# Opening loads of a Mamba-2 and hard-swish kernel: two issuing queues, and the first weight block decoded ahead of C's transpose

## The chip, the cores and the metric

The kernel runs on one core of a Trainium2 chip. The metric is the device time of one execution in microseconds; the figure given for a kernel is the median of its runs. The profile is one execution, recorded on the same core. Its span runs from the first to the last instruction.

## The reference: what is computed

Two blocks follow each other. The first is a chunked state-space recurrence over 4 batches, 8 heads and 768 tokens, with 32 values and 16 states per head:

```python
log_a = np.log(np.clip(a, 1e-06, 1.0))
for c in range(nc):
    cum = np.cumsum(la, axis=-1)
    L = np.exp(cum[:, :, :, None] - cum[:, :, None, :]) * causal
    CB = np.einsum('bhin,bhjn->bhij', Cc, Bc)
    y_intra = np.einsum('bhij,bhjd->bhid', CB * L, xc)
    y_inter = np.einsum('bhin,bhnd->bhid', Cc, state) * np.exp(cum)[:, :, :, None]
    y[:, :, sl] = y_intra + y_inter
    state = decay_full * state + (sum over j of Bc, xc, decay_from_j)
```

The result, 3072 tokens by 256 features, goes through a feed-forward block with 2048 hidden features:

```python
h = x @ w_in
g = h * np.clip(h + 3.0, 0.0, 6.0) / 6.0
return (g @ w_out).astype(np.float32)
```

The two weight matrices come as 64-bit floats; all other inputs are 32-bit.

## The kernel before, in words

**Tiling.** The sequence is cut into six chunks of 128 tokens; one chunk of all four batches is 512 tokens. For each chunk c the recurrence gives yT (256 features by 512 tokens), and the feed-forward block of group k = c turns it into 512 rows of the output. The recurrence of chunk k + 1 is woven into the feed-forward work of group k. Groups 1 to 5 do both matrix products with seven block products in place of eight, from sums of weights and of activations; group 0 does them plainly (`mlp_in` at L608, `first_out` at L698).

**Order.** Nothing is scheduled automatically: every engine and every DMA queue does its work in the order of the program text. Semaphores between them are put in by the framework. Transfers raise one of eight DMA semaphores in turn, and a transfer whose semaphore is still in use by an earlier one waits for that one to land. In the kernel before, all transfers are issued by SP.

**Weights.** The weights are decoded on the core. Each matrix is loaded in four blocks of 1 MB of raw 64-bit words (`load_w`, L128), into three buffers in turn (`raw`). In the text, w0 to w3 are the blocks of w_in, blocks 4 to 7 those of w_out. `decode(i)` (L188) is a generator of five steps, and `weights(i, n)` takes n of them:

- ScalarE copies the top 16 bits (`ws`, L199); for blocks 0 and 1 VectorE also builds the significand (`wm`, L202 and L206) in this step.
- VectorE cuts exponent and sign (`we`, L216, and `ws`, L218); for later blocks L202 follows.
- ScalarE turns the exponent into a bfloat16 factor (`we`, L222).
- ScalarE does so a second time (L224); for later blocks VectorE does L206; and the load of block i + 3 is issued.
- VectorE adds the sign (L229) and writes the 32-bit weights (`w_in` or `w_out`, L237).

**The opening.** Chunk 0 has a path of its own, since nothing precedes it. SP loads a, w0, C in eight transfers of 32 KB (`pairs_first`, L96), B in one transfer of 4096 pieces of 64 bytes (`tokens_first`, L91), and x in 4096 pieces of 128 bytes. Meanwhile the logarithms of a are taken (L265, L267), added up by a scan (L270) and split into three bfloat16 parts. TensorE forms the decay differences of chunks 0 and 1 in PSUM (`diff`: L349 and L358), and ScalarE takes their exponentials into L (`diff_exp`, L366). C is transposed by VectorE in blocks of 32 (`turn_squares`, L464) and spread over even and odd heads (`part_heads`, L470). B is transposed by TensorE (`turn_b`, L428; ScalarE copies the result to bT, L432) and scaled by GpSimd (`ends`, L392, into `bs`). `scores` (L506) multiplies them into cb, `multiply` (L553) puts cb into L, `mix` (L578) multiplies L with x, and `keep` (L598) copies the result to yT by four copies on ScalarE. `fade` (L477) scales the second half of C by the decay, for the part of `mix` that reads the state in the chunk's middle. `turn_cum` and `by_token` (L315, L319) put the later chunks' decay sums on partitions, through a PSUM bank (`c_ps`, tag f1) that the second half of `mix` writes next.

**Where w1 is asked for.** `load_w(1, behind=...)` at L882 first has GpSimd copy one column of L into the new buffer (L132). So the transfer waits until `multiply` has written that part of L. Blocks 2 and 3 are issued right after.

Of the kernel before, what the change touches and what calls it, by code (L numbers as in the profile page):

```python
# [8 lines left out]
FP32 = mybir.dt.float32  # L9
# [11 lines left out]
def kernel(  # L21
# [63 lines left out]
    def load_bc(c):  # L85

        sl = slice(c * P, (c + 1) * P)

        def tokens_first(src, **where):  # L91
            t = loads.tile([P, NB * NH, N], FP32, **where)
            nc.sync.dma_start(out=t, in_=src[:, :, sl, :].rearrange("b h s n -> s (b h) n"))
            return t

        def pairs_first(src):  # L96
            t = loads.tile([P, 2, NB, 4, N], FP32, name="pairs", tag="bc")
            for b in range(NB):
                for h in range(2):
                    nc.sync.dma_start(  # L100
                        out=t[:, h, b].rearrange("s a n -> s (a n)"),
                        in_=src[b, h:NH:2, sl, :].rearrange("h (s a) n -> h s (a n)", a=4))
            return t

        if c == 0:
            bcs[c] = [pairs_first(C)]
        elif c < TURN:
            bcs[c] = [tokens_first(C, name="C", tag="bc")]
        Bs[c] = tokens_first(B, name="B")
        if c < TURN:  # L110
            bcs[c].append(Bs[c])
        else:
            bcs[c] = [pairs_first(C), pairs_first(B)]

    def load_x(c):
        sl = slice(c * P, (c + 1) * P)
        xts[c] = loads.tile([P, NB * NH, D], FP32, name="xt")
        nc.sync.dma_start(out=xts[c], in_=x[:, :, sl, :].rearrange("b h s d -> s (b h) d"))
# [6 lines left out]
    NRAW = 3  # L125
    raws = {}

    def load_w(i, behind=None):  # L128

        raw = loads.tile([P, NK * FP * 2 * P], U32, name="raw", bufs=NRAW)  # L130
        if behind is not None:
            nc.gpsimd.tensor_copy(raw[:, :1].bitcast(FP32), behind)  # L132
        if i < NP:
            cols = slice(2 * i * FP * P, 2 * (i + 1) * FP * P)
            src = moe_w_in[:, cols].rearrange("(k p) f -> p k f", p=P)
            dst = raw.rearrange("p (k f) -> p k f", k=NK)
        else:
            r0 = (i - NP) * FP * P
            src = moe_w_out[r0:r0 + FP * P, :].rearrange("(k p) m -> p k m", p=P)
            dst = raw.rearrange("p (k m) -> p k m", k=FP)  # L140
        nc.sync.dma_start(out=dst, in_=src)
        raws[i] = raw

    load_w(0)
    load_bc(0)
    load_x(0)
    nc.scalar.preload_act_table_set("natural_log_exp_and_others")


# [38 lines left out]
    def decode(i):  # L188

        n = NK * FP * P
        top = raws[i].bitcast(U16).rearrange("p (n w) -> p n w", w=4)[:, :, 3]
        lo, hi = (raws[i].rearrange("p (n w) -> p n w", w=2)[:, :, w] for w in range(2))
        s = att.tile([P, n], U16, name="ws")
        e = att.tile([P, n], U16, name="we")
        m = att.tile([P, n], U32, name="wm")
        nc.scalar.copy(out=s, in_=top)  # L199

        def significand():
            nc.vector.tensor_scalar(  # L202
                out=m, in0=hi, scalar1=0xFFFFF, scalar2=0x100000,
                op0=ALU.bitwise_and, op1=ALU.bitwise_or)
            yield
            nc.vector.scalar_tensor_tensor(  # L206
                out=m.bitcast(FP32), in0=lo, scalar=2.0 ** -32, in1=m, op0=ALU.mult,
                op1=ALU.add)
            yield

        parts_m = significand()
        if i < 2:
            next(parts_m)
            next(parts_m)
        yield
        nc.vector.tensor_scalar(  # L216
            out=e, in0=s, scalar1=0x7FF0, scalar2=None, op0=ALU.bitwise_and)
        nc.vector.tensor_scalar(  # L218
            out=s, in0=s, scalar1=0x8000, scalar2=None, op0=ALU.bitwise_and)
        next(parts_m, None)  # L220
        yield
        nc.scalar.activation(e.bitcast(BF16), e, AF.Relu, bias=bias_hi, scale=-8.0)  # L222
        yield
        nc.scalar.activation(e, e.bitcast(BF16), AF.Relu, bias=bias_lo, scale=-1.0)  # L224
        next(parts_m, None)
        if i and i + NRAW < 2 * NP:
            load_w(i + NRAW)
        yield
        nc.vector.tensor_tensor(out=e, in0=e, in1=s, op=ALU.bitwise_or)  # L229
        m, e = m.bitcast(FP32), e.bitcast(BF16)  # L230
        if i < NP:
            dst = w_in[:, :, i * FP * P:(i + 1) * FP * P]
            m, e = (t.rearrange("p (k f) -> p k f", k=NK) for t in (m, e))
        else:
            dst = w_out[:, (i - NP) * FP:(i - NP + 1) * FP, :]
            m, e = (t.rearrange("p (k f) -> p k f", k=FP) for t in (m, e))
        nc.vector.scalar_tensor_tensor(  # L237
            out=dst, in0=m, scalar=2.0 ** -20, in1=e, op0=ALU.mult, op1=ALU.mult)
# [30 lines left out]
    def add_up(sl):  # L269
        nc.vector.tensor_tensor_scan(  # L270
            out=cum[:, sl], data0=run.rearrange("g c p -> g (c p)")[:, sl], data1=a_sb[:, sl],
            initial=0.0, op0=ALU.mult, op1=ALU.add)
# [90 lines left out]
    def diff_exp(c, b):  # L363
        if c not in Ls:
            new_decays(c)
        nc.scalar.activation(Ls[c][:, b], ds.pop((c, b)), AF.Exp)  # L366

    def first_eto():

        e_ps = ps.tile([P, NB, HT], FP32, name="e_ps", tag="f0")  # L370
        for b in range(NB):
            nc.tensor.matmul(
                out=e_ps[:, b],
                lhsT=picks[:, b * P:(b + 1) * P],
                rhs=split[:, 0, HALF[1]], start=(b == 0), stop=True, skip_group_check=True)
        etos[0] = att.tile([P, NB, P], FP32, name="eto")
        nc.scalar.activation(etos[0][:, :, HALF[1]], e_ps, AF.Exp)
# [14 lines left out]
    def ends(c, b):  # L392

        if b == 0:
            bss[c] = att.tile([P, G, N], FP32, name="bs")
        hs = slice(b * NH, b * NH + NH)
        nc.gpsimd.tensor_tensor(  # L397
            out=bss[c][:, hs], in0=Bs[c][:, hs],
            in1=Ls[c][:, b, :, HT - 1:HT].to_broadcast([P, NH, N]), op=ALU.mult)
# [8 lines left out]
    def turned(c):  # L408
        if c not in bTs:
            bTs[c] = [att.tile([P, NB, P], FP32, name="bT", bufs=1),  # L410
                      att.tile([P, NB, 2, P], FP32, name="cT", bufs=1),
                      att.tile([P, NB, P], FP32, name="csT", bufs=1)]
        return bTs[c]
# [14 lines left out]
    def turn_b(c):  # L428

        t_ps = turn_ps(c, 1)  # L430
        transposes(c, 1, t_ps)
        nc.scalar.copy(out=turned(c)[0], in_=t_ps)  # L432
# [31 lines left out]
    def turn_squares(t, out):  # L464

        nc.vector.transpose(
            out=out.rearrange("r b (s a) -> r b a s", a=4),
            in_=t.rearrange("s t b a n -> s (b a) t n"))

    def part_heads(c):  # L470
        _, cT, csT = turned(c)
        for t in range(2):
            nc.vector.tensor_scalar(
                out=cT[:, :, t], in0=csT, scalar1=parity[:, t:t + 1], scalar2=None,
                op0=ALU.mult)

    def fade(c, sl=slice(0, P)):  # L477
        csT = turned(c)[2][:, :, sl]
        nc.vector.tensor_tensor(out=csT, in0=csT, in1=etos[c][:, :, sl], op=ALU.mult)

    def turn_all(c):
        bT, _, csT = turned(c)
# [358 lines left out]
    def weights(i, n):  # L841
        for _ in range(n):
            next(parts[i], None)


    def diff(c, *bs):
        for part in (diff_less, diff_pick):
            for b in bs:
                part(c, b)
# [10 lines left out]
        mask_again(0, b)  # L860
    diff(0, 0, 1)
    diff(0, 2, 3)
    turn_squares(bcs[0][0], turned(0)[2])
    part_heads(0)
    for b in range(NB):
        diff_exp(0, b)
    first_eto()
    weights(0, 1)
    add_up(ends_at[1])
    store_rows()  # L870
    diff(1, 2, 3)
    turn_b(0)
    for b in range(NB):
        ends(0, b)
    weights(0, 1)
    diff(1, 0, 1)
    diff_exp(1, 2)
    diff_exp(1, 3)
    weights(0, 2)
    scores(0)  # L880
    multiply(0)
    load_w(1, behind=Ls[0][:, 0, 2, :1])  # L882
    load_w(2)
    load_w(3)
    c_ps = ps.tile([P, NC, G], FP32, name="c_ps", tag="f1")
    turn_cum(c_ps)
    by_token(c_ps)
    busy(1, ps.tile([P, NB * P], FP32, name="d", tag="f0"))
    fade(0, HALF[1])
    weights(0, 1)  # L890
    mix(0)
    keep(0)
    weights(1, 2)
    renew(0)
    weights(1, 3)
    load_eto(1)
    load(1)

# [136 lines left out]
```

## Time and profile before

| what | us |
|---|---|
| median of 3 runs | 363.7 (362.79 to 363.85) |
| profiled execution, its span | 361.1 |
| TensorE matmul busy | 349.9 |
| VectorE busy | 223.3 |
| ScalarE busy | 177.2 |
| GpSimd busy | 139.5 |
| first matmul of the up projection (h, L611) starts | 23.46 |
| first matmul of the down projection (o, L708) starts | 53.77 |

The runs' times are taken without the profiler and include what lies around the span, here 2.6 us between the span and the median. PE is TensorE's matmuls, PEld its weight loads, DVE is VectorE, ACT ScalarE, POOL GpSimd; SPq is SP's queue of transfers. A line of a timeline has the start, the length and the engine, then the line of the code, the operation, output<-inputs and a count, and in brackets how long the engine had been idle before it and what ended that wait. In the chain of waits each piece is released by the one above it.

### The profile page before, as it was taken

The page shows a single profiled execution, that of the slowest core. Times are in us where ns is not written, and L with a number is a line of the kernel's source. Part 1 is how long each engine was busy: PE and PEld are TensorE (multiplying, and loading weights), DVE is VectorE, ACT ScalarE, POOL GpSimd, SP SyncE. Part 2 cuts the span into 40 slices and gives each one's busy share as a digit, 9 for nine tenths or more (in the row PEclk, how much of TensorE's full clock was granted, in tenths as well). Part 3 has the DMA queues.
Part 4 walks back from the last instruction along what each step waited for, and adds up shares of the span by engine and source line. Part 5 has one row for each costly group of instructions (what it writes and reads, how often), then busy time and mean ns, then how long its engine had stood idle before and what let it go on. Part 6 is the DMA issues. An engine that isn't in the chain of part 4 may idle for free.

```text
span 361.1 us, 9354 instructions
## 1 busy us (share of the span) xinstructions
PE 349.9 (97%) x3936; PEld 300.4 (83%) x3936; DVE 223.3 (62%) x427; ACT 177.2 (49%) x390; POOL 139.5 (39%) x139
## 2 busy tenths in 40 slices
PE   7698999999999999999999999999999999999996
PEld 3553438888888999888999888999888999888996
DVE  4778999976787634587435587535588421588111
ACT  4548878439656550575460476470476110476100
POOL 3400000182299712079722079720058700058700
PEclk9699999999999999999999999999999999999999
DMA  5979969901935043560034560000000000000000
GB/s 154 109 270 254 145 230 156 172 2 43 181 55 77 4 98 91 72 93 2 2 76 104 79 96 2 4 2 31 29 2 1 4 2 31 30 3 0 2 29 31
DMA packets 75482, 24.97 MB, mean 69 GB/s; under 512 B 66032, under 2 KB 71824, under 8 KB 74928
## 3 DMA queue, kind: packets, MB, share of 16 engines
q1 hardware_dynamic: 75440, 24.37, 34.7%
q8 instruction: 31, 0.51, 0.6%
q14 instruction: 11, 0.09, 0.1%
HBM read 21.07 MB, written 3.29 MB: 67 GB/s over the span
## 4 chain that ended last, share of the span: by engine, by line
PE 76%; DVE 13%; ACT 4%; DMA 3%; SPq 2%; issue 1%; DVEq 0%; POOL 0%; ACTq 0%
PE ob L767 18%; PE even L653 18%; PE oa L767 18%; PE odd L653 13%; DVE gT L694 2%; DVE wm L206 2%; PE o L708 2%; PE y L589 2%; PE cb L523 2%; PE y L501 2%; ACT we L222 2%; SPq L100 2%; DMA raw<-in_moe_w_in_dram 2%; DMA B<-in_B_dram 1%; DVE w_out L237 1%; DVE we L229 1%
## 5 line engine op out<-in xcount | busy, mean ns | idle before, releaser
L753 POOL TENSOR_TENSOR s<-gT 128x512 f32<-128x512 f32 x20 | 26.4, 1321 | 89.5 <-DVE gT L694 89.5
L653 PE MATMUL even<-ts,w_sum 128*128 128x256 f32 x160 | 48.2, 383 | 0.0
L668 ACT COPY even<-odd 128x512 f32<-128x512 f32 x40 | 23.0, 576 | 48.6 <-PE odd L653 46.3
L689 ACT ACTIVATE gT<-odd,half 128x512 f32<-128x512 f32 x40 | 27.5, 687 | 35.0 <-DVE odd L682 35.0
L653 PE MATMUL odd<-yT,w_in 128*128 128x256 f32 x160 | 41.1, 379 | 0.0
L767 PE MATMUL oa<-w_out,gT 128*128 128x128 f32 x320 | 38.9, 277 | 0.0
L767 PEld LDWEIGHTS oa<-w_out,gT 128*128 128x128 f32 x320 | 38.1, 192 | 0.9
L767 PE MATMUL ob<-w_out,s 128*128 128x128 f32 x320 | 37.4, 275 | 0.0
L767 PEld LDWEIGHTS ob<-w_out,s 128*128 128x128 f32 x320 | 36.5, 192 | 0.0
L653 PEld LDWEIGHTS even<-ts,w_sum 128*128 128x128 f32 x160 | 29.9, 190 | 5.3 <-ACT up L675 1.5
L694 DVE SCALAR_TENSOR_TENSOR gT<-gT,odd 128x512 f32<-128x512 f32 x40 | 27.5, 688 | 9.9 <-ACT gT L689 9.9
L653 PEld LDWEIGHTS odd<-yT,w_in 128*128 128x128 f32 x160 | 30.1, 190 | 3.9
L386 ACT ACTIVATE L<-L,cum_n 128x64 f32<-128x64 f32 x128 | 31.1, 339 | 0.0
L767 PE MATMUL ob<-t,gT 128*128 128x128 f32 x240 | 30.3, 279 | 0.0
L611 PE MATMUL h<-yT,w_in 128*128 128x512 f32 x64 | 28.4, 599 | 1.9 <-DVE gT L694 1.6
L689 ACT ACTIVATE gT<-even,half 128x512 f32<-128x512 f32 x40 | 27.7, 694 | 4.4 <-PE even L653 4.4
L694 DVE SCALAR_TENSOR_TENSOR gT<-gT,even 128x512 f32<-128x512 f32 x40 | 27.1, 679 | 4.4 <-ACT gT L689 4.4
L767 PEld LDWEIGHTS ob<-t,gT 128*128 128x128 f32 x240 | 27.9, 192 | 1.2 <-issue 0.5
L708 PE MATMUL o<-w_out,gT 128*128 128x256 f32 x128 | 28.7, 381 | 0.0
L669 DVE COPY up<-odd 128x256 f32<-128x256 f32 x40 | 17.0, 424 | 18.7 <-ACT even L668 17.9
L708 PEld LDWEIGHTS o<-w_out,gT 128*128 128x128 f32 x128 | 24.0, 190 | 4.0 <-ACT gT L689 0.8
L397 POOL TENSOR_TENSOR bs<-B,L 128x128 f32<-128x128 f32 x24 | 14.5, 612 | 31.6 <-ACT L L386 23.5
(130 smaller groups left out, 614.9 us busy)
## 6 DMA issues: line engine op xcount, KB each, us to landing
raw<-in_moe_w_in_dram SPq DMA_DIRECT2D x4, 1024.0 KB
raw<-in_moe_w_out_dram SPq DMA_DIRECT2D x4, 1024.0 KB
L<-cum_d SPq DMA_DIRECT2D x8, 512.0 KB
xt<-in_x_dram SPq DMA_DIRECT2D x6, 512.0 KB
out_dram<-res SPq DMA_DIRECT2D x20, 128.0 KB
B<-in_B_dram SPq DMA_DIRECT2D x6, 256.0 KB
eto<-cum_e SPq DMA_DIRECT2D x20, 64.0 KB
pairs<-in_C_dram SPq DMA_DIRECT2D x32, 32.0 KB
```

What stands on the lines that cost most here:

```text
L100: nc.sync.dma_start(out=t[:, h, b].rearrange("s a n -> s (a n)"), in_=src[b, h:NH:2, sl, :].rearrange("h (s a) n -> h s (a n)", a=4))
L386: nc.scalar.activation(Ls[c][:, b, h], Ls[c][:, b, h], AF.Exp, bias=cum_n[:, c, g:g + 1])
L397: nc.gpsimd.tensor_tensor(out=bss[c][:, hs], in0=Bs[c][:, hs], in1=Ls[c][:, b, :, HT - 1:HT].to_broadcast([P, NH, N]), op=ALU.mult)
L611: nc.tensor.matmul(out=h.rearrange("p r i -> p (r i)"), lhsT=w_in[:, j, f * P:(f + 1) * P], rhs=yTs[k][:, j].rearrange("p b i -> p (b i)") ...
L653: nc.tensor.matmul(out=bank[:, r], lhsT=lhsT, rhs=rhs, start=start, stop=True, skip_group_check=True)
L668: nc.scalar.copy(out=even, in_=odd[:, 1:2].to_broadcast([P, 2, 2 * P]))
L669: nc.vector.tensor_copy(out=up[:, 1], in_=odd[:, 0])
L689: nc.scalar.activation(gTs[k][:, f], h.rearrange("p r i -> p (r i)"), AF.Relu, bias=half, scale=1.0 / 6.0)
L694: nc.vector.scalar_tensor_tensor(out=g, in0=g, scalar=1.0, in1=h.rearrange("p r i -> p (r i)"), op0=ALU.min, op1=ALU.mult)
L708: nc.tensor.matmul(out=o[:, b % 2], lhsT=gTs[0][:, f, b * P:(b + 1) * P], rhs=w_out[:, f], start=(f == 0 and b % 2 == 0), stop=True, skip_ ...
L753: nc.gpsimd.tensor_tensor(out=o, in0=p_, in1=q_, op=op)
L767: nc.tensor.matmul(out=bank[:, slot], lhsT=lhs[:, j], rhs=rhs[:, j], start=(clear and j == 0), stop=True, skip_group_check=True)
```

## The change

The change has five parts.

- **Two queues.** w0 and chunk 0's B are issued by ScalarE, ahead of its activation table load; a, C, x and then w1 by SP. In SP's order the load of w1 now stands behind x, without the copied column, and the loads of blocks 2 and 3 before and after `scores` and `multiply`.
- **First decoding moved.** Block 0's first two steps of `decode` (ScalarE's copy of the top bits; VectorE's significand, exponent and sign) now stand ahead of the exponentials and of C's transpose. Its third step stands ahead of chunk 1's exponentials.
- **Second block's decoding.** Only block 0 builds its significand in the first step; block 1 does so as the later blocks do. Its first step stands ahead of `keep`, so ScalarE does that copy before the four yT copies. Its next three steps stand between `keep` and `renew`, and the last one behind `renew`.
- **`by_token` moved.** It stands behind block 0's last step.
- **`fade` of chunk 0 moved.** It is done by GpSimd, right behind C's `part_heads` in the text and, on GpSimd, behind the four operations of `ends`.

TensorE's order is the same as before.

```diff
-        def tokens_first(src, **where):
+        def tokens_first(src, queue=nc.sync, **where):
             t = loads.tile([P, NB * NH, N], FP32, **where)
-            nc.sync.dma_start(out=t, in_=src[:, :, sl, :].rearrange("b h s n -> s (b h) n"))
+            queue.dma_start(out=t, in_=src[:, :, sl, :].rearrange("b h s n -> s (b h) n"))
...
+        if 0 < c < TURN:
+            bcs[c] = [tokens_first(C, name="C", tag="bc")]
+        Bs[c] = tokens_first(B, nc.scalar if c == 0 else nc.sync, name="B")
         if c == 0:
-            bcs[c] = [pairs_first(C)]
+            bcs[c] = [pairs_first(C), Bs[c]]
         elif c < TURN:
-            bcs[c] = [tokens_first(C, name="C", tag="bc")]
-        Bs[c] = tokens_first(B, name="B")
-        if c < TURN:
             bcs[c].append(Bs[c])
...
-    def load_w(i, behind=None):
+    def load_w(i, queue=nc.sync):
         raw = loads.tile([P, NK * FP * 2 * P], U32, name="raw", bufs=NRAW)
-        if behind is not None:
-            nc.gpsimd.tensor_copy(raw[:, :1].bitcast(FP32), behind)
...
-        nc.sync.dma_start(out=dst, in_=src)
+        queue.dma_start(out=dst, in_=src)
...
-    load_w(0)
+    load_w(0, nc.scalar)
     load_bc(0)
     load_x(0)
+    load_w(1)
     nc.scalar.preload_act_table_set("natural_log_exp_and_others")
...
         parts_m = significand()
-        if i < 2:
+        if i == 0:
...
-    def fade(c, sl=slice(0, P)):
+    def fade(c, sl=slice(0, P), engine=nc.vector):
         csT = turned(c)[2][:, :, sl]
-        nc.vector.tensor_tensor(out=csT, in0=csT, in1=etos[c][:, :, sl], op=ALU.mult)
+        engine.tensor_tensor(out=csT, in0=csT, in1=etos[c][:, :, sl], op=ALU.mult)
...
     diff(0, 2, 3)
-    turn_squares(bcs[0][0], turned(0)[2])
-    part_heads(0)
+    weights(0, 1)
     for b in range(NB):
         diff_exp(0, b)
     first_eto()
+    diff(1, 2, 3)
     weights(0, 1)
+    for b in range(NB):
+        ends(0, b)
+    turn_b(0)
+    diff(1, 0, 1)
+    weights(0, 1)
+    diff_exp(1, 2)
+    diff_exp(1, 3)
+    turn_squares(bcs[0][0], turned(0)[2])
+    part_heads(0)
+    fade(0, HALF[1], nc.gpsimd)
     add_up(ends_at[1])
     store_rows()
-    diff(1, 2, 3)
-    turn_b(0)
-    for b in range(NB):
-        ends(0, b)
+    load_w(2)
     weights(0, 1)
-    diff(1, 0, 1)
-    diff_exp(1, 2)
-    diff_exp(1, 3)
-    weights(0, 2)
     scores(0)
     multiply(0)
-    load_w(1, behind=Ls[0][:, 0, 2, :1])
-    load_w(2)
     load_w(3)
     c_ps = ps.tile([P, NC, G], FP32, name="c_ps", tag="f1")
     turn_cum(c_ps)
+    busy(1, ps.tile([P, NB * P], FP32, name="d", tag="f0"))
+    weights(0, 1)
+    weights(1, 1)
     by_token(c_ps)
-    busy(1, ps.tile([P, NB * P], FP32, name="d", tag="f0"))
-    fade(0, HALF[1])
-    weights(0, 1)
     mix(0)
     keep(0)
-    weights(1, 2)
+    weights(1, 3)
     renew(0)
-    weights(1, 3)
+    weights(1, 1)
```

## The prediction, made blind

> **What bounds the kernel now.** I read the page first, then the chain of waits in order of time, then the timelines of single queues and engines in the first 80 us, and last a table of DMA and clock by stretch. The page's chain says where the span lies:
>
> ```profile
> PE 76%; DVE 13%; ACT 4%; DMA 3%; SPq 2%; issue 1%; DVEq 0%; POOL 0%; ACTq 0%
> ```
>
> From 77 us on the chain is TensorE without a gap, work that the change doesn't touch. What is to be had lies before it. There the chain runs (start, length, what):
>
> ```profile
> 7.63 5.02 DMA B<-in_B_dram
> ...
> 12.79 1.09 PE t_ps L423 x4
> ...
> 15.72 2.06 PE cb L523 x64
> ...
> 19.14 0.20 POOL raw L132
> ...
> 19.35 5.43 DMA raw<-in_moe_w_in_dram
> ...
> 24.81 0.70 DVE wm L202
> ```
>
> B's landing at 12.65 releases its transposes and, through them, the scores (cb). The scores' end releases the multiplications into L (17.79). Only then is the second weight block (w1) asked for, and it lands at 24.79. B is late because SP's queue issues one transfer after another:
>
> ```profile
> 0.80 0.40 SPq L80 DMA_DIRECT2D pre<-in_a_dram  x1
> 1.26 0.41 SPq L141 DMA_DIRECT2D raw<-in_moe_w_in_dram  x1
> 1.73 5.86 SPq L100 DMA_DIRECT2D pairs<-in_C_dram  x8
> 7.63 0.47 SPq L93 DMA_DIRECT2D B<-in_B_dram  x1
> 8.15 3.28 SPq L118 DMA_DIRECT2D xt<-in_x_dram  x1
> ```
>
> C is as late as B for its own reader, VectorE, which idles 4.43 us ahead of it, while ScalarE copies w0 only after the decay exponentials:
>
> ```profile
> 10.71 1.08 DVE L466 STREAM_TRANSPOSE csT<-pairs 128x512 f32<-128x512 f32 x1 [4.43 <-DMA pairs<-in_C_dram]
> ```
>
> TensorE idles from 10.0 to 12.79, and its clock is halved from 12.0 to 18.7 (columns: stretch, length, busy of PE, PEld, DVE, ACT, POOL, then clock, DMA share, GB/s):
>
> ```profile
> 8.00:10.00 2.00, 2.00 (x71) 1.40 (x70) 0.00 (x0) 1.92 (x5) 0.00 (x0) 1.00 0.94 115
> 10.00:12.00 2.00, 0.01 (x2) 0.00 (x0) 1.26 (x2) 0.85 (x1) 0.00 (x0) 1.00 0.89 69
> 12.00:14.00 2.00, 1.21 (x5) 1.00 (x6) 1.97 (x4) 0.09 (x1) 1.20 (x2) 0.50 1.17 175
> ```
>
> From 23.46 TensorE does the first group's up projection (h), then its down projection (o), which ends near 75.6:
>
> ```profile
> 23.46 7.13 PE L611 MATMUL h<-yT,w_in 128*128 128x512 f32 x16
> 32.17 14.14 PE L611 MATMUL h<-yT,w_in 128*128 128x512 f32 x32 [1.58 <-DVE gT L694]
> 46.67 7.13 PE L611 MATMUL h<-yT,w_in 128*128 128x512 f32 x16 [0.36 <-DVE w_in L237]
> 53.77 15.78 PE L708 MATMUL o<-w_out,gT 128*128 128x256 f32 x72
> ```
>
> Two gaps stand in it, 1.58 and 0.36, both waits for the decoded weights. VectorE's chain (decoding, gT) and TensorE's arrive together at 75.7, where csT is ready. So the whole must gain on both: TensorE from an earlier start of h and from the gaps, VectorE from an earlier w1.
>
> **What the Trainium skill says.** "DMA: Bandwidth & Descriptors", section "Issuing engines are not separate DMA queues": transfers of all queues run on the same 16 DMA engines, and a second queue saves only issue time. The trace agrees that issue is what costs: the ten transfers from C on take until 11.43 to issue. Section "Queues, rings and completion order" there: the DMA engines take turns between queues by packet; all early loads of this trace are on one queue, so it isn't shown. "TensorE: Matmul & The Clock Gate", section "What's actually happening": the clock halves after an idle window of about 3.4 us. Here 2.0 us of idle were enough (10.0 to 12.0), and the measurement counts. "SBUF — State Buffer", section "SBUF: two separate sides": GpSimd and a VectorE operation with two SBUF inputs exclude each other; bs (L397) took 587 to 1390 ns each beside VectorE's decoding, which agrees.
>
> **The change, part by part.** Times are from the span's start; those after are estimates from the rows named.
>
> *ScalarE's two issues* (0.41 and 0.47 as on SP) stand ahead of the table load of 1.28: 0.80 to 3.0. Its next work, Ln, began at 3.14 waiting for VectorE. Cost nothing, with 0.1 of cover.
>
> *w0* is issued 0.46 earlier. Before, the rates by stretch add up to it and a (1.15 MB) at 5.9; it had landed by 7.06, when SP issued a C transfer that waits for w0's semaphore. Five C transfers now run beside it (160 KB, 0.4 us at the peak of 414 GB/s). Bounds 5.9 to 8; I take 6.8.
>
> *C.* In the changed order the sixth C transfer waits for w0's semaphore: 6.85 plus three issues of 0.54 is 8.5. From issue to use took 2.0 (a: 0.80 to 2.83) at least, and 3.1 for the last C before (7.59 to 10.71): 10.5 to 11.6. I take 10.7, no gain. This is why moving w0 away doesn't bring C forward.
>
> *w0's copy ahead of the exponentials:* 6.8 to 7.95; the four exponentials (2.25) end at 10.2 instead of 9.6, eto at 10.6. *w0's first decoding ahead of C's transpose:* 0.69 + 1.22 + 0.56 + 0.52 from 6.8, with the copy in between, ends at 9.8. Both lie in the wait for C; without that cover they would cost 3.0.
>
> *B* follows w0 on ScalarE's queue, from 6.0: 2.5 at the rate of its own transfer (issue to landing 5.02 less some 2.5 behind C) to 5.0: 8.5 to 11.0, I take 9.5. TensorE is then idle under 1.5 us, the clock stays up, and B's transposes, their copy and chunk 1's differences (0.6 + 0.59, 1.25) are done near 12.
>
> *Scores.* C's transpose and cT (1.08 + 0.88) end at 12.7. cb takes 1.2 at full clock (the next chunk's row), to 13.9; the second scan (1.42) lets VectorE start L at 14.1 instead of 17.79: 3.7 earlier. On GpSimd bs ends by 13.5 (bound 15.0 with B at 11.0), and the fade that it takes over costs 0.62 to 0.87 (L404, same size) for 0.41 on VectorE; it is due 3.7 after L's start. Cost nothing. The removed copy into raw saves 0.2 in a place that no longer counts.
>
> *cum_n moved behind w0's last two steps* (0.72 + 1.23): its bank is written next by the second half of mix. It ends 4.7 after L's start, and that half began 4.3 after it: plus 0.5. So h starts 5.67 + 0.5 = 6.2 after L: 20.3 for 23.46, gain 3.2.
>
> *w1* is issued behind x, near 8.6. x moves until 13.0 (3.3 us in the table of rates); w1 needs 2.6 at 400 GB/s up to 5.43 as now: 15.6 to 18.4. Its copy (1.15) stands ahead of the four yT copies on ScalarE. Up to 18.4 that costs nothing: 18.4 + 1.15 + two yT copies of 0.37 is 20.3. The rest of its decoding starts at 18.8 on VectorE (3.8), waits for ScalarE's two steps behind yT (20.8 to 23.1), and w_in's second part is done at 25.1 instead of 31.5. TensorE needs it at 20.3 + 7.1 = 27.4. Both gaps go: 1.9. Of the later blocks, w2 and w3 are issued near 14.5 instead of 20; VectorE has gained 6.4 against TensorE's 5.1, so TensorE sets the pace to 75 us, and everything behind shifts whole.
>
> Sum: 3.2 + 1.9 = 5.1. The profiled span of 361.1 becomes 356.0; some 2.6 lie between it and the median of 363.7 (runs 362.79 to 363.85), so 358.6. With w0, C and B at their bounds the gain is 6.2 to 4.0: 357.5 to 359.7.
>
> **Rivals.** *w1 late:* two queues share the engines, w1 lands at 21, and ScalarE's yT copies stand behind its copy: h at 21 + 1.9 = 22.9, gain 0.6 + 1.9: 361.2. For it: w1 is last in SP's queue. Against: from 15 to 20 the DMA engines moved 39 GB/s, so there is room.
>
> *w0 and C late:* packets of C and a slow w0 by turns put w0 at 9, C at 13; TensorE idles past 2 us and runs at half clock: cb 15.0 to 17.1, h at 23.3, gain 0.2 + 1.9: 361.6. For it: C's last three transfers now hang on w0. Against: w0 had the engines at up to 414 GB/s before, and C is a quarter of its bytes.
>
> *ScalarE held, slower:* SP was held 1.61 us at its fifth C and 3.28 at x, while earlier transfers drained. If B's issue (4096 pieces of 64 bytes) is held on ScalarE until w0 has drained at 5.9, the table load ends at 7.2 and Ln starts 4.1 late; TensorE idles from 6 to 10.4, at half clock until some 6 us of work later; 3.7 us of differences end at 17.1, B's transposes, differences and cb (0.6, 1.25, 1.2) at 20.2, h at 26.4: minus 2.9 plus 1.9, 364.7. It decides from a hold to about 4.9, where h comes at 25.4. Against: at 30.44 SP's C load of the same 4096 pieces issued in 0.54 behind a weight block in flight.
>
> *No effect:* VectorE's chain from 24.8 to 75.7 gives the gain back, by waits for gT: 363.5. Against: its work is only shifted.
>
> **How the numbers follow.** Forecast 0.64; w1 late 0.10; w0 and C late 0.12; held 0.06; no effect 0.04; better than 357.3 0.04. From 357.3 to 361.7 holds 0.86 of it. A measurement here can tell 0.3% (1.1 us) from no change: faster 0.90, within 0.04, slower 0.06.
>
> **What would show it.** In the profile after: C's transpose near 10.7; no half clock between 12 and 18; L's first multiplication near 14; h at 20 without the two gaps; w_in's second part near 25; the same work behind 77 us, 5 us earlier. Wrong if Ln moves past 4, if yT copies wait for w1, or if C lands past 12.

## The result and the profile after

| what | before, us | after, us |
|---|---|---|
| median of 7 runs each, side by side | 363.7 (362.79 to 363.85) | 360.31 (359.41 to 363.42) |
| profiled execution, its span | 361.1 | 357.9 |
| h starts | 23.46 | 23.29 |
| h starts to o starts | 30.31 | 27.57 |
| o starts to the next chunk's first L500 | 21.97 | 21.69 |

The ratio is 0.9921, with an interval of 0.9895 to 0.9947: 3.4 us faster, where the forecast was 5.1. In every execution the time is the span plus 1.65 to 1.9. The profiled execution of before took 362.8 (a quick one of its kind) and that of after 359.6; the table splits the 3.2 between these two.

The chain of waits of the changed kernel, in order of time (start, length, what):

```profile
0.80 5.83 DMA raw<-in_moe_w_in_dram
6.63 0.02 issue
6.65 0.61 SPq L100
...
8.56 4.29 DMA pairs<-in_C_dram
...
13.03 1.10 DVE csT L465
...
14.16 0.89 DVE cT L472 x2
...
15.19 2.12 PE cb L522 x64
...
17.31 1.30 DVE L L563 x2
```

Before, B stood in this place of the chain. Now it is C, which lands at 12.85 and not in time for a use at 10.7. Behind it come C's transpose, cT and cb, and L's multiplication begins at 17.31 instead of 17.79. At h's start 0.17 of this is left, and that is all that the opening won. TensorE in the changed kernel:

```profile
15.19 2.01 PE L522 MATMUL cb<-cT,bT 32*64 32x128 f32 x64 [2.42 <-DVE cT L472]
...
23.29 27.73 PE L610 MATMUL h<-yT,w_in 128*128 128x512 f32 x64
50.86 15.70 PE L707 MATMUL o<-w_out,gT 128*128 128x256 f32 x72
```

The 64 multiplications of h stand in one piece: both gaps, 1.58 and 0.36, are gone. In the first line TensorE has waited 2.42 for cT, and cb takes 2.01. The windows of the same kernel (columns as in the prediction) give the reason in the clock:

```profile
12.00:14.00 2.00, 0.76 (x33) 0.58 (x32) 0.97 (x1) 2.00 (x4) 0.61 (x2) 1.00 1.51 168
14.00:16.00 2.00, 0.81 (x32) 0.84 (x40) 1.97 (x4) 1.39 (x2) 0.82 (x1) 0.77 0.96 196
16.00:18.00 2.00, 2.00 (x111) 1.67 (x96) 0.85 (x3) 0.00 (x0) 0.69 (x1) 0.50 0.98 387
```

It falls to half at 15.07, 2.3 us after TensorE ran dry at 12.76; in the kernel before it fell at 12.01, 2.0 after. And this is why C is late, in windows of 1 us of the same kernel:

```profile
4.00:5.00 1.00, 1.00 (x4) 0.34 (x3) 1.00 (x5) 0.75 (x2) 0.21 (x1) 1.00 1.02 397
...
7.00:8.00 1.00, 0.56 (x4) 0.14 (x4) 0.97 (x2) 0.75 (x1) 0.00 (x0) 1.00 1.49 108
8.00:9.00 1.00, 1.00 (x35) 0.67 (x34) 0.97 (x2) 0.54 (x2) 0.00 (x0) 1.00 0.38 43
```

Up to 5.6 the engines move w0, at 397 GB/s from 4 to 5. C was issued from 1.27 on by another queue, and in the packet records nothing of it moves before 6.03, when w0's last packet is through (5.96) and B's first pieces have begun (5.59). At 7 to 8 the engines are full (a share of 1.49) with 108 GB/s: the 64-byte pieces of B. C's first four transfers take about 0.9 each beside them, the last four 0.5, and its last packet is through at 11.97. Before, all eight took 0.5 (5.5 to 9.5), and B came after them.

### The profile page after: what moved, and what is told of

The parts are those of the page before. It is cut to its first block, busy times and chain, and to the rows that moved or that the text cites. A ratio compares the mean times of both kernels' runs of the same rounds, so it can differ in the third digit from the quotient of the medians.

```text
span 357.9 us, 9350 instructions
## 1 busy us (share of the span) xinstructions
PE 347.9 (97%) x3936; PEld 300.0 (84%) x3936; DVE 221.9 (62%) x426; ACT 177.5 (50%) x390; POOL 137.9 (39%) x139
## 3 DMA queue, kind: packets, MB, share of 16 engines
q1 hardware_dynamic: 71056, 23.06, 33.9%
## 4 chain that ended last, share of the span: by engine, by line
PE 91%; DVE 3%; DMA 3%; ACT 1%; SPq 1%; issue 0%; DVEq 0%; ACTq 0%
PE ob L766 18%; PE even L652 18%; PE oa L766 18%; PE odd L652 13%; PE o L707 8%; PE h L610 8%; PE y L588 3%; PE y L500 2%; PE cb L522 2%; DMA raw<-in_moe_w_in_dram 2%; DMA pairs<-in_C_dram 1%; PE y L534 1%; SPq L100 1%; DVE odd L681 0%; DVE up L668 0%
## 5 line engine op out<-in xcount | busy, mean ns | idle before, releaser
L652 PEld LDWEIGHTS even<-ts,w_sum 128*128 128x128 f32 x160 | 29.9, 190 | 5.3 <-ACT up L674 1.5
L563 DVE TENSOR_TENSOR L<-L,cb 128x512 f32<-128x512 f32 x24 | 15.3, 681 | 18.0 <-PE cb L522 15.5
```

Of the source, the lines that this page charges most:

```text
L563: nc.vector.tensor_tensor(out=Ls[c][:, :, hs], in0=Ls[c][:, :, hs], in1=cbs[c][q], op=ALU.mult)
L652: nc.tensor.matmul(out=bank[:, r], lhsT=lhsT, rhs=rhs, start=start, stop=True, skip_group_check=True)
```

## The experiments

The theory after the result: (1) the gain is w1's early load and the new order of block 1's decoding; (2) the opening gave almost nothing because C, not B, is late now, by B's pieces beside it and not by the semaphore of w0; (3) the half clock then took what was left. Rivals: the second queue itself gains; C's semaphore wait is what holds it; the clock doesn't matter. Kernels of one batch are compared with runs of the kernel before in that batch (medians 363.0, 362.9 and 363.2).

**w1's load alone.** The kernel before, with

```diff
     load_x(0)
+    load_w(1)
...
-    load_w(1, behind=Ls[0][:, 0, 2, :1])
```

> The kernel before with one edit: w1's load is issued behind x instead of behind the multiplication into L. Theory (the gain of the change is w1's arrival, which takes the waits for decoded weights out of the up projection): h starts near 23.5 as before, the gaps of 1.58 and 0.36 and the small ones are gone, h to o takes 27.6 instead of 30.3; ratio to before about 0.992, like the changed kernel. Rival (the gain comes from two queues and from the earlier decoding of w0, and w1 merely follows): ratio 0.997 to 1.000.

Median 362.27, ratio 1.0009 (0.9973 to 1.0045): no gain that can be told. The profiled execution (361.26) had lost the gap of 1.58; from h to o it took 28.56 instead of 30.31. But four of eleven runs took 365.5 to 366.3, all with a mean granted clock of 0.986, against 361.1 to 362.4 at 0.99 and above. So the load wins the gap in this execution, and the four runs at the lower clock take it back in the ratio. What such a mean clock stands for is worked out under the clock below.

**The two queues alone.** The kernel before, with

```diff
-    load_w(0)
+    load_w(0, queue=nc.scalar)
...
-        Bs[c] = tokens_first(B, name="B")
+        Bs[c] = tokens_first(B, nc.scalar if c == 0 else nc.sync, name="B")
```

> The kernel before with one edit: w0 and chunk 0's B are issued by ScalarE, all else is left. Theory (the second queue doesn't bring C forward; C waits until w0 has passed and then shares the engines with B's 4096 pieces): C's transpose starts near 13.0 instead of 10.7, although B lands before 11; L's first multiplication near 19.5 instead of 17.8; slower than before by 1.5 to 2.5 us, ratio 1.004 to 1.007. Rival (two queues help, since B no longer stands behind C): L's first multiplication before 17.5, ratio 0.992 to 0.999.

Median 363.69, ratio 1.0023 (1.001 to 1.0037): slower by 0.7, where 1.5 to 2.5 was expected. C's transpose starts at 12.96 (before 10.71), L at 18.64 (17.79), h at 24.30 (23.46). A second queue gains nothing here by itself; it trades an early C for an early B (used from 11.13 on GpSimd, before 12.80).

**B alone on ScalarE.** The changed kernel, with w0 back on SP:

```diff
-    load_w(0, nc.scalar)
+    load_w(0)
```

> The changed kernel with w0's load moved back to SP, ahead of C; only B is issued by ScalarE. Theory (C's lateness comes from B's pieces passing between C's once w0 is through, not from w0 being on the other queue): B, ahead of w0's packets, is through by 6; C's transpose starts near 11, TensorE doesn't fall to half clock, L's first multiplication near 15 and h near 21; 2 to 2.5 us faster than the changed kernel, ratio to before 0.985. Rival (C is late because any second queue in front of it blocks it): C's transpose near 13 again, ratio as the changed kernel, 0.992.

Median 362.88, ratio 0.9993 (0.9965 to 1.0022). Its runs lie between 360.2 (clock 0.995) and 365.8 (0.975). C's transpose came at 13.88, later still. Its chain of waits:

```profile
0.80 9.00 DMA B<-in_B_dram
...
9.82 0.53 SPq L100
```

Here the sixth transfer of C needed B's semaphore and was issued at 9.82. So the theory's forecast failed in this kernel (C's transpose near 11, a gain of 2 to 2.5): the semaphore that the prediction feared for w0 does hold C when it is B's, which lands late. In the changed kernel that wait is for w0 and costs little (issue at 6.65, 6.85 in the prediction).

**B behind C.** The changed kernel, with B on SP again:

```diff
-        Bs[c] = tokens_first(B, nc.scalar if c == 0 else nc.sync, name="B")
         if c == 0:
-            bcs[c] = [pairs_first(C), Bs[c]]
+            bcs[c] = [pairs_first(C)]
+        Bs[c] = tokens_first(B, name="B")
+        if c == 0:
+            bcs[c].append(Bs[c])
```

> The changed kernel with B's load moved back to SP behind C; w0 alone is issued by ScalarE. Theory (C is late in the changed kernel because its transfers run at half pace, 0.9 us each instead of 0.5, between B's pieces, once w0 is through; that w0 is on the other queue does no harm and no good): C's eight transfers follow each other at 0.5 us from about 5.6, C's transpose starts at 10.7 instead of 13.0; B lands at 12.5 to 13. TensorE then idles for B instead, and the time stays within 1 us of the changed kernel. Rival (C is held up by w0 on the other queue, or by the semaphore that its sixth transfer waits for): C's transpose stays later than 12.

VectorE of this kernel, and its windows at the stretch where the changed kernel had 1.49 and 108 GB/s:

```profile
11.09 1.08 DVE L467 STREAM_TRANSPOSE csT<-pairs 128x512 f32<-128x512 f32 x1 [0.73 <-DMA pairs<-in_C_dram]
```

```profile
7.00:8.00 1.00, 0.37 (x2) 0.11 (x2) 0.96 (x3) 0.55 (x1) 0.00 (x0) 1.00 0.33 63
```

Without B beside it C moves at 0.5 per transfer and is there 1.9 us earlier, though w0 is still on the other queue. That shows cause (2). The time doesn't follow: B now lands at 13.75, TensorE waits 2.58 for it, and the median is 364.57, ratio 1.0039 (1.0016 to 1.0061), 4.3 above the changed kernel where at most 1 was expected. In the profiled execution, a quick one (361.47), L begins at 17.76, and TensorE stalls for 1.04 in the products L times x. Its runs spread from 361.5 to 365.9, those from 364.6 on with a clock of 0.984 to 0.986.

**Fillers for the clock.** The changed kernel, with two matmuls that nobody reads in the wait for C (the profile shows each as two):

```diff
     diff(1, 0, 1)
+    busy(2, ps.tile([P, NB * P], FP32, name="d", tag="f2"))
```

> The changed kernel with two added matmuls of the identity (no use is made of the result) on TensorE in its idle time between chunk 1's differences and the scores. Theory (the half clock from 14.5 to 18 costs time on the path: cb 2.0 instead of 1.2, the products with x 1.18 instead of 0.86): the clock stays full, L's first multiplication 0.8 us earlier (16.5), h near 22.5; 0.8 us faster than the changed kernel, ratio to before 0.990. Rival (the path at this point is VectorE's scan and ScalarE, not TensorE): L's start moves under 0.3 us, ratio 0.992.

Median 359.31 (358.74 to 359.61), ratio 0.9897 (0.9879 to 0.9915): 1.0 below the changed kernel (0.9 by the ratios, whose intervals overlap), and its runs lie within 0.9 where the changed kernel's span 4.0. TensorE in it:

```profile
15.21 1.20 PE L522 MATMUL cb<-cT,bT 32*64 32x128 f32 x64 [0.39 <-DVE cT L472]
16.33 0.86 PE L534 MATMUL y<-xt,bs 64*32 64x64 f32 x64
...
22.44 2.84 PE L610 MATMUL h<-yT,w_in 128*128 128x512 f32 x6
```

cb takes 1.20 for 2.01, and h comes 0.85 earlier, while C's transpose starts as in the changed kernel (13.00 and 13.03). This shows cause (3).

**`by_token` back to the front.** The changed kernel, with `by_token` ahead of block 0's last two steps:

```diff
+    by_token(c_ps)
     weights(0, 1)
     weights(1, 1)
-    by_token(c_ps)
```

> The changed kernel with cum_n computed right behind the multiplication into L, as in the kernel before, ahead of w0's last two steps. Theory (the second half of mix waits for cum_n to free its bank): that half no longer waits, h starts 0.3 to 0.5 us earlier; ratio to before 0.990 to 0.991. Rival (the decoding of block 1 sets the pace of the up projection, so h's start is worth nothing): ratio as the changed kernel, 0.992.

Median 359.67, ratio 0.9914 (0.9898 to 0.993). The comparison is spoilt: in the profiled execution TensorE stood idle for 2.19 and the clock stayed full all the same (cb 1.20), and then its products L times x stalled for 1.35 without a releaser that the profile shows. Both are taken up below. The same edit on top of the fillers:

> The changed kernel with two fillers, and the copy of the decay sums (by_token) ahead of w0's last two steps on VectorE. Theory: the second half of the products L times x then waits neither for the clock nor for that copy, h starts 0.6 to 0.9 earlier (21.6 to 21.8 instead of 22.44), and the median goes from 359.3 to 358.4 to 358.8. Rival: w0's last step, two tenths later, or an unexplained stall of TensorE in those products (1.35 when the copy was moved without fillers) takes the place: within 0.3 of 359.3 or above.

Median 359.21, ratio 0.9907 (0.9889 to 0.9924), beside 359.31: the rival was right, the place of `by_token` is worth nothing that these runs can tell. (The profiled execution is the slowest of its six, 360.64: there TensorE came to full clock only at 11.46, so L began at 17.56.)

**C ahead of the weights.** SP issues a, C, w0, x, w1; ScalarE only B, behind its table load; block 0 is decoded behind C's transpose, and block 1's first step stands behind `keep` again:

```diff
-    load_w(0, nc.scalar)
+    nc.scalar.preload_act_table_set("natural_log_exp_and_others")
     load_bc(0)
+    load_w(0)
     load_x(0)
     load_w(1)
-    nc.scalar.preload_act_table_set("natural_log_exp_and_others")
...
```

> The changed kernel with the opening loads in the order of their need: SP issues a, C, w0, x, w1; ScalarE issues B alone, behind the table load; the first steps of w0's decoding stand behind C's transpose again, the last ones behind the multiplication into L. Theory (the opening is bound by C, and by x and w0 after it): C's transpose starts near 8 to 9, before TensorE runs out of work, no half clock between 12 and 14; L's first multiplication at 14.5, x lands near 15, h near 20.5; 2.5 to 3 us faster than the changed kernel, ratio to before 0.984. Rival (whatever comes first, w0 or x comes too late in its place): h not before 22, ratio 0.988 to 0.992.

C's transpose started at 9.85 and cb at 12.03, but TensorE then waited 3.28 for x, which is behind w0; half clock followed until 29.9. Median 364.37, ratio 1.004 (1.0024 to 1.0056). With x ahead of w0, and all of w0's decoding behind the multiplication into L:

> As the one before, with x ahead of w0 in SP's order and all of w0's decoding behind the multiplication into L. Theory: L's first multiplication at 13.5, x in time, w0 lands near 15 and its decoding ends near 21; h near 21.3, ratio to before 0.986. Rival (w0 late holds up h further): h not before 22.5, ratio 0.990 or more.

L began at 13.74, as early as the prediction had promised, and still the median was 362.4, ratio 0.9979 (0.997 to 0.9988). TensorE of this kernel says where it went:

```profile
16.50 0.95 PE L585 MATMUL y<-L,xt 64*32 64x64 f32 x62
20.75 0.30 PE L585 MATMUL y<-L,xt 64*32 64x64 f32 x2 [3.30 <-issue]
```

3.30 was lost in the middle of the products. Half clock from 21.3 to 28.1 followed; h started at 23.94 and took 29.63 to o instead of 27.57. Stalls like it, of 0.2 to 3.3, stand in seven of the fourteen kernels behind the 56th to 62nd of these 64 matmuls, so at about one place in TensorE's instructions. The profile lists a DMA queue for instructions, and its packets fit: every kernel has one of 16 KB on this queue in this stretch. In the seven with a stall TensorE goes on 1.3 to 1.6 after the packet is through (here 19.11 and 20.75). In the seven without, it was through at least 1.4 ahead of the 62nd matmul (19.14 and 20.81 in the changed kernel, which loads at 408 GB/s there all the same). In this longest stall the packet moved only from 18.17 on, 0.7 into the stall, while the weight blocks loaded at some 400 GB/s. So these two matmuls most likely waited for their instructions, and those behind the weight blocks; no run tests it by an edit.

**A ladder at full clock.** Three kernels to price the parts with the clock kept. The first is the kernel before with three fillers:

```diff
     diff(1, 2, 3)
+    busy(3, ps.tile([P, NB * P], FP32, name="d", tag="f1"))
     turn_b(0)
```

> The kernel before with three matmuls without a reader ahead of B's transposes on TensorE. This is the clock's part alone. Theory: in the kernel before, TensorE stands still from 10.0 to 12.8 and has half clock from 12 to about 18.5; with the three matmuls (10.0 to 11.7) the clock stays full, cb takes 1.2 instead of 2.0 and the products with x 0.86 instead of 1.19. But VectorE reaches L's multiplication only behind its two steps of w0 at 17.05 (before 17.79), so not more than 0.7 is won: h at about 22.7, median 362.9 to 363.2. w1's load follows L, so the gap before w_in's second part is unchanged at 1.4 to 1.6. Rival: the clock costs as much in the kernel before as it did in the changed one (1.0); then 362.4 or less.

Median 362.52, ratio 0.9989 (0.9979 to 0.9998); h at 23.06. The clock was 1.000, but L still began at 17.40, now behind GpSimd's bs, and the first gap stayed (1.29). That is between theory and rival: the clock is worth 0.4 (by the ratio) to 0.7 (by the medians) in the kernel before. The second adds w1's early load:

> The same with w1's load right behind x's and no copied column: the load's part alone, with the clock kept. Theory: the 1.6 to 1.7 us that the span won with w1's early load under an uncertain clock come out in the median now: 361.2 to 361.5, no gap before w_in's second part, up projection 28.6 long. Rival: the early load disturbs as much as it helps (as its median of 362.3 beside 362.9 suggested): 362.3 or more.

Median 362.08 (360.69 to 363.3), ratio 0.9972 (0.996 to 0.9984): 0.4 less in the median, where the theory had 1.0 to 1.3. The profiled execution, the quickest of its 18, had no first gap; why the others are slower by up to 2.6 (1.8 at a clock of 1.000), no trace here shows. The third gives block 1's decoding the changed kernel's order:

```diff
-        if i < 2:
+        if i == 0:
...
+    weights(1, 1)
     mix(0)
     keep(0)
-    weights(1, 2)
+    weights(1, 3)
     renew(0)
-    weights(1, 3)
+    weights(1, 1)
```

> The same with block 1's decoding in the changed kernel's order (its first step ahead of the yT copies, its significand later, the last step behind renew). Theory: this is where the up projection goes from 28.6 to 27.6, so about 1.0 less than the kernel with w1's load alone: 360.2 to 360.5. Then the two queues and w0's decoding moved ahead are worth the rest to the changed kernel with two fillers (359.31): about 1. Rival: the shortening from 28.6 to 27.6 came with the earlier end of w0's decoding; then this one stays within 0.3 of the kernel with w1's load alone.

Median 360.58, ratio 0.9946 (0.9925 to 0.9966): 1.5 less again (0.9 between the two profiled executions). TensorE's h without and with that order, the second kernel first:

```profile
23.11 21.12 PE L612 MATMUL h<-yT,w_in 128*128 128x512 f32 x48
44.58 7.13 PE L612 MATMUL h<-yT,w_in 128*128 128x512 f32 x16 [0.36 <-DVE w_in L238]
```

```profile
23.59 27.73 PE L612 MATMUL h<-yT,w_in 128*128 128x512 f32 x64
```

The last gap goes with the decoding's order, not with the load: VectorE starts block 1's exponents at 22.19 instead of 24.65, as ScalarE has copied w1 ahead of yT, and finishes w_in's second part at 28.3 instead of 29.4. The blocks behind it come earlier too.

The ladder by medians, with the changed kernel's fillers as its last step: before 363.2, clock 362.5, w1 early 362.1, its decoding spread 360.6, all the rest (queues, block 0's decoding, `fade`, `by_token`, the places of the loads of blocks 2 and 3) 359.3. So w1's load and decoding are worth 1.9 of 3.9, the larger part but not all of it as theory (1) had it: with the clock kept the rest is worth 1.3, with h at 22.44 instead of 23.59. The changed kernel without fillers loses 1.0 to the clock. The steps come from two batches, and by the intervals of the ratios they are uncertain by 0.4 to 1.0 each.

## Why the prediction was right, and where not

The sign and the range were right; the size was 5.1, and 3.4 was measured. That the time fell into the range is in part luck: the larger of the two terms, 3.2 from the opening, came as 0.17, and the time lies in the range because that reached to 361.7 to take in the rivals, and because the smaller term came larger than forecast. Two of the three things that the prediction named as signs of being wrong came: Ln moved past 4, and C landed past 12. In the profiled executions the span is 1.9 above the forecast of 356.0: h 3.0 later than predicted, the gaps 0.8 better, o 0.3 shorter. By the prediction's steps:

- **ScalarE's two issues, cost nothing: right in effect.** B's issue took 0.49 and was not held. Ln did pass 4 (4.25 instead of 3.14), but because a landed 1.1 later beside w0, which the prediction had not costed. It didn't matter, since C was later still.
- **w0 at 6.8: right,** 6.63 to 6.65.
- **C in use at 10.7: the step that failed.** It read the semaphore rightly: SP waited 0.2 for w0, and the sixth transfer was issued at 6.65. But the three last issues took until 9.34 (2.7 instead of 1.6), and from there to the use it was 3.7 instead of the 2.0 to 3.1 of the kernel before, because B's pieces, from the other queue, were ahead of C and beside it. The bound of 11.6 was missed by 1.4. The prediction priced C beside w0, where nothing of it moved, and C behind w0's semaphore, but never C beside B.
- **TensorE idle under 1.5, clock full: failed** as a consequence: 2.42 idle, cb at 2.01 instead of 1.2, the products with x 1.18 instead of 0.86. L came at 17.31 and not 14.1: 2.3 of this is C, the other 0.9 came behind it, 0.8 of that in cb.
- **B at 9.5: late, without harm.** Its last piece moved at 10.57, and its transposes ran at 11.08 without a wait, just past the bound of 11.0.
- **w0's copy and first decoding hidden in the wait for C: right.** VectorE still waited 2.86 for C behind them. They pay only with the clock kept, where L begins at 16.46.
- **`fade` on GpSimd: mis-sized but harmless.** 1.50 instead of 0.62 to 0.87, from 15.18 to 16.68 beside VectorE's second scan (14.96 to 16.16), which the prediction had not set against it; 4 us ahead of its reader.
- **h 6.2 behind L: right,** 5.98. Together the gain in h was 0.17 instead of 3.2.
- **w1 and the gaps: right, and undersized.** w_in's second part was done at 28.0 (31.5 before); both gaps went. The term was 1.9 and measured 2.74 in the profiled executions, with 0.28 more behind o: besides the gaps, the matmul time of h was 28.40 in three pieces and 27.73 in one. The ladder's medians give w1 and its decoding 1.9, so how far the term was too small stays open.
- **2.6 between span and median: mis-sized.** It is 1.65 to 1.9 in every execution; the profiled one of before was 0.9 below its median. For the changed kernel 357.9 + 1.7 is 359.6, 0.7 below the median, by the clock of the single runs (0.980 to 0.995).

The rival "w0 and C late" had the times (C 13, L 17.1, h 23.3) and the half clock, but by another cause: w0 was not late. "w1 late" failed: yT was not held up. "ScalarE held" failed at its point of decision, B's issue.

**The clock.** The Trainium skill, "TensorE: Matmul & The Clock Gate", section "What's actually happening", gives an idle window of about 3.4 us; here less halved the clock (2.0 in the kernel before, 2.13 with the two queues alone, 2.3 in the changed kernel), and 2.19 with `by_token` in front did not. The clock's changes in the traces explain the odd one. In each of the fourteen they lie 3.41 us or a multiple of it apart (before: 5.19, 12.01, 18.84; changed kernel: 4.83, 15.07, 18.48; C and x ahead of w0: 7.64, 21.30, 28.12), so they fall on the edges of windows of 3.41 us. The eight windows that ended with the clock halved held 2.01 to 3.41 of idle; no other window at full clock held more than 1.8. The 2.19 lay across an edge at 13.98, 0.93 before and 1.26 behind it.

Where the edges lie differs from trace to trace, so an idle of some 2 us costs the clock in one run and not in another. Halved, the clock stayed so for one, two or four windows in these traces. By an estimate from these figures one such window lowers the mean clock by 0.0047 (half of 3.41 in 360): the changed kernel's runs at 0.995, 0.990 and 0.980 then had one, two and four of them, with times of 359.4 to 359.9, 360.3 to 360.7 and 363.4. The four late runs of w1's load alone (0.986) had three, by the same estimate.

## What to carry to other kernels

Moving loads to a second queue brought one of them forward here (B, used at 11.1 instead of 12.8) and set another back by 2.3 (C), since both now shared the engines. So price each early transfer beside the one that now runs next to it, small pieces above all. When the last input of a short phase moves by a microsecond, look at TensorE's idle time first: two matmuls without a reader were worth about 1.0 us here, and made the runs agree. To forecast a median, take what lies around the span from an execution whose span and time are both known, not from another run's median.

## What the runs showed of the hardware

- A load issued on SP's queue at 1.27 moved nothing until w0, issued on ScalarE's at 0.80, was nearly or wholly through (6.03 against 5.96 in the changed kernel, 5.44 against 6.02 with the two queues alone), though a, issued on SP at 0.80, did move beside w0 and was 1.1 late. The Trainium skill, "DMA: Bandwidth & Descriptors", section "Queues, rings and completion order", has the engines take turns between queues by packet. B's pieces and C did so (0.9 per transfer of 32 KB instead of 0.5); C and w0 did so at most in w0's last 0.6; why, no run here shows.
- The same two-input operation of 128x256 on GpSimd took 1.50 in the changed kernel, beside VectorE's scan, and 0.72 in the kernel with B behind C, where VectorE stood idle.
- A half clock may last: with C first and x behind w0 it went from 16.3 to 29.9. A stall of 1.00 lies inside it, but none in its last two windows, so what kept it up stays open.
